# Order of the last second products, and the engines that copy and send the last rows, in a fused attention and ELU-MLP kernel

## The chip, the cores and the metric

The kernel runs on one core of one Trainium2 chip. The metric is the device time of one execution in microseconds (us); medians are over separate executions.

## The reference

The first half is sliding-window attention over 8 batches, 8 heads, 576 positions and 64 dimensions. The second is a two-layer MLP with an ELU between, on 4608 tokens:

```
x = attention(q, k, v)                  # window 32, softmax; (4608, 512)
h = x @ w_in                            # (4608, 2048)
g = where(h > 0, h, exp(min(h, 0)) - 1)
out = g @ w_out                         # (4608, 512) fp32
```

## The kernel before

The MLP runs in 144 steps: 18 tiles of 256 tokens, each in 8 steps of 256 hidden columns. One step is a first product (`mm1`, into PSUM), ScalarE's exponential, two VectorE operations that make g, and, two steps later, the second product (`mm2`), which adds into two PSUM tiles (the prediction says banks): `psY[t][0]` for the first 128 rows of the tile (called ts0 here, "upper rows") and `psY[t][1]` for the other 128 (ts1, "lower rows"). The attention is woven between the steps. In the very last step the first product is cut into two halves, so that g comes in two halves as well.

```python
def mm2(kk, parts=(0, 1)):
    t, s = order[kk]
    ...                                       # (cut) psY[t] allocated at s == 0
    for ts in parts:
        for j in range(FG):                   # FG = 2
            nc.tensor.matmul(psY[t][ts],
                lhsT=g_t[kk][:, j, ts * 128:(ts + 1) * 128],
                rhs=w_out_sb[:, s * FG + j, :], ...)
    if last and s == STEPS - 1:               # the last tile's rows
        for ts in parts:
            for z in range(1 + ts):           # ts0 whole, ts1 in two halves
                c = slice(z * D_MODEL // 2 * ts,
                          D_MODEL if z == ts else D_MODEL // 2)
                eng = (nc.vector, nc.scalar)[z]
                y_sb = opool.tile([128, D_MODEL], FP32,
                                  tag=f"y_sb{1 - z}", name="y_sb")
                copy_on(eng, y_sb[:, c], psY[t][ts][:, c])
                (nc.scalar if z else nc.sync).dma_start(
                    out_t[t, :, ts, c], y_sb[:, c])
    ...                                       # (cut) the other tiles' stores
```

The loop runs step 142's product in two parts, one part before each part of step 143's: 142 ts0, 143 ts0, 142 ts1, 143 ts1.

The softmax here doesn't subtract the row's maximum and nothing guards it: scores larger than these inputs give would overflow.

## Time and profile before

| | before |
|---|---|
| time, median of 3 runs | 305.11 us (304.83 to 305.93) |
| span of the profiled run | 304.5 us |
| TensorE busy | 296.0 us, 97% |
| start of ScalarE's last two exponentials to span end ("the tail", defined below) | 6.91 us |
| last packet of the stores to landing of the last store | 0.34 us |

The prediction below shows the engines' shares, the tail in order of time and the DMA engines' load. One part of the page that it does not show matters later. It is in the list of DMA queues over the whole span, of which these are the last three lines (packets, MB, share of 16 engines' time):

```profile
q10 hardware_dynamic: 1872, 6.62, 5.8%
q8 instruction: 24, 0.39, 0.6%
q14 instruction: 11, 0.09, 0.1%
```

q10 is ScalarE's queue; q1, left out here, is SyncE's (from 300.3 us on q10 moved 0.13 MB, ScalarE's one store of 128 KB, and q1 0.39 MB, SyncE's two). The packets of kind "instruction" I read as fetches of the engines' own program, since the experiments below move them by adding instructions to an engine (eight on ScalarE, one of q14 by some 6 us).

**A measure for the tail.** The body of the kernel scatters by some two microseconds from run to run (the moment at which the last step's first half exponential starts lay between 296.3 and 298.4 us in the 19 traces of this study). So all times of the tail are given from that moment, which I call the marker: the start of the first of ScalarE's last two 128x256 exponentials (297.56 us in this trace). "Tail" is from the marker to the end of the span.

### The profile page before, as it was taken

Reading aid. Unit: us, or ns where it says so; the run is one execution under the profiler, and the core shown is the slowest. Engines: PE = TensorE matmul, PEld = TensorE weight load, DVE = VectorE, ACT = ScalarE, POOL = GpSimd, SP = SyncE. Lnnn points to the kernel's source line nnn. Section 1 sums busy time; section 2 is a strip of 40 time slices with the busy share of each in tenths; the row PEclk is TensorE's granted clock in tenths of the full one; section 3 lists DMA queues with packets and bytes.
Section 4 is the critical chain, followed back from the end, with each engine's and each line's share of the span. In section 5 each row is a group of like instructions: output and inputs, shape, how many; then the busy total and the mean of one; then the engine's idle time right before and its main releaser. Section 6 shows DMA issues by size and latency. Waiting matters only on the chain.

```text
span 304.5 us, 7644 instructions
## 1 busy us (share of the span) xinstructions
PE 296.0 (97%) x3091; PEld 197.4 (65%) x3091; DVE 242.2 (80%) x473; ACT 168.6 (55%) x254; POOL 48.6 (16%) x68
## 2 busy tenths in 40 slices
PE   8789999999999999999999999999999999999995
PEld 3456666677676666666666666666667666666662
DVE  6867688978888887988798879887988787877664
ACT  3654556778664567546754675467535353534331
POOL 8836100910003100230013001400000000000000
PEclk9999999999999999999999999999999999999999
DMA  9999999998755997999799969996921111111011
GB/s 191 177 201 205 183 272 413 295 168 182 177 176 158 297 126 187 246 319 157 164 251 303 196 157 268 325 159 116 281 57 71 34 71 34 72 37 69 2 69 70
DMA packets 92117, 52.81 MB, mean 173 GB/s; under 512 B 76594, under 2 KB 81970, under 8 KB 92082
## 3 DMA queue, kind: packets, MB, share of 16 engines
q1 hardware_dynamic: 47330, 35.61, 43.3%
q0 software_dynamic: 42880, 10.10, 40.9%
q10 hardware_dynamic: 1872, 6.62, 5.8%
q8 instruction: 24, 0.39, 0.6%
q14 instruction: 11, 0.09, 0.1%
HBM read 36.70 MB, written 15.34 MB: 171 GB/s over the span
## 4 chain that ended last, share of the span: by engine, by line
PE 90%; DMA 3%; DVE 2%; POOL 2%; ACT 1%; issue 1%; DVEq 0%; POOLq 0%; ACTq 0%
PE ps L602 41%; PE psY L640 40%; PE psS L336 4%; PE psS L304 3%; DMA w_in_sb<-in_moe_w_in_dram 3%; PE ptx L279 1%; POOL Ve L142 1%; POOL c L136 1%; PE psXT L357 1%; DVE g_sb L626 1%; ACT pu L315 1%; DVE pm L324 0%; DVE m_sb L615 0%; PE ptx L274 0%; ACT e_sb L609 0%
## 5 line engine op out<-in xcount | busy, mean ns | idle before, releaser
L609 ACT ACTIVATE e_sb<-ps 128x512 f32<-128x512 f32 (+1 forms) x145 | 86.3, 595 | 120.6 <-PE ps L602 113.0
L602 PE MATMUL ps<-xT,w_in_sb 128*128 128x256 bf16 x1152 | 149.2, 273 | 1.4 <-DMA w_in_sb<-in_moe_w_in_dram 1.4
L640 PE MATMUL psY<-w_out_sb,g_sb 128*128 128x512 bf16 x576 | 147.6, 380 | 0.2 <-DVE g_sb L626 0.2
L602 PEld LDWEIGHTS <-w_in_sb 128*128 128x128 bf16 x1152 | 110.6, 98 | 39.7 <-DMA w_in_sb<-in_moe_w_in_dram 1.9
L626 DVE SCALAR_TENSOR_TENSOR g_sb<-ps,m_sb 128x512 bf16<-128x512 f32 (+1 forms) x145 | 99.4, 686 | 12.6
L615 DVE TENSOR_SCALAR m_sb<-e_sb 128x512 bf16<-128x512 f32 x144 | 62.5, 434 | 38.3 <-ACT e_sb L609 36.5
L640 PEld LDWEIGHTS <-g_sb 128*128 128x128 bf16 x576 | 54.5, 98 | 39.0 <-DVE g_sb L626 0.6
L142 POOL DMA_DIRECT2D Ve<-in_v_dram x40 | 35.4, 897 | 139.7 <-PE psS L336 79.9
L315 ACT ACTIVATE pu<-psS 128x1024 bf16<-128x1024 f32 x36 | 36.5, 1021 | 1.4 <-PE psS L304 1.4
L348 DVE TENSOR_TENSOR x_st<-psS,rc 128x512 bf16<-128x512 f32 x36 | 24.9, 692 | 1.2
L324 DVE TENSOR_TENSOR pm<-pu,masks 128x1024 bf16<-128x1024 bf16 x36 | 24.6, 683 | 0.6 <-ACT pu L315 0.5
L234 ACT CAST qkb<-f 128x768 bf16<-128x768 f32 (+1 forms) x29 | 25.0, 860 | 0.0
L336 PEld LDWEIGHTS <-pm 128*64 128x64 bf16 x576 | 11.2, 111 | 9.9 <-DVE pm L324 8.7
L336 PE MATMUL psS<-Ve,pm 128*64 128x65 bf16 x320 | 13.6, 197 | 0.9 <-DVE pm L324 0.9
L236 DVE COPY y_sb<-psY 128x512 f32<-128x512 f32 (+1 forms) x19 | 12.7, 671 | 1.0 <-PE psY L640 1.0
L304 PEld LDWEIGHTS <-kT 64*128 64x128 bf16 x576 | 9.5, 95 | 4.9 <-issue 4.0
L336 PE MATMUL psS<-Vo,pm 128*64 128x65 bf16 x256 | 12.0, 196 | 0.2 <-DVE Vo L153 0.2
L304 PE MATMUL psS<-qT,kT 64*128 64x64 bf16 x576 | 11.8, 191 | 0.5 <-DVE kT L236 0.5
L234 ACT COPY y_sb<-psY 128x512 f32<-128x512 f32 (+1 forms) x18 | 10.3, 571 | 3.0 <-DVE y_sb L236 3.0
L153 DVE COPY Vo<-Ve 64x1040 bf16<-64x1040 bf16 x24 | 10.3, 431 | 1.5 <-DMA Ve<-in_v_dram 0.8
L395 PE MATMUL ps_idle<-zeros 128*128 128x512 bf16 x27 | 9.5, 482 | 1.3 <-DVE zeros L194 1.3
L234 ACT COPY qT<-ptx 128x1152 bf16<-128x1152 bf16 (+2 forms) x8 | 7.5, 971 | 3.9 <-PE ptx L279 3.0
(36 smaller groups left out, 72.4 us busy)
## 6 DMA issues: line engine op xcount, KB each, us to landing
out_dram<-y_sb SPq DMA_DIRECT2D x35, 256.0 KB, 3.5
f<-in_q_dram SPq DMA_DIRECT2D x12, 576.0 KB, 5.6
f<-in_k_dram SPq DMA_DIRECT2D x12, 576.0 KB, 7.9
in_dram<-qkb ACTq DMA_DIRECT2D x10, 576.0 KB, 3.9
Ve<-in_v_dram POOLq DMA_DIRECT2D x24, 128.0 KB, 11.0
w_in_sb<-in_moe_w_in_dram POOLq DMA_DIRECT2D x4, 512.0 KB, 9.9
w_out_sb<-in_moe_w_out_dram POOLq DMA_DIRECT2D x4, 512.0 KB, 12.8
Ve<-in_v_dram POOLq DMA_DIRECT2D x16, 96.0 KB, 10.5
```

Source lines behind the costliest of these rows:

```text
L142: nc.gpsimd.dma_start(out=V_e[b % 3][p0:p1, m, :, 0:D], in_=v[b, :, lo + p0:lo + p1, :].rearrange("h p d -> p h d"))
L234: nc.scalar.copy(d_, s_)
L304: nc.tensor.matmul(psS[:, h % 2, hp * 128 + z * QB:hp * 128 + (z + 1) * QB], lhsT=kT[b % 2][base:base + 64, KPAD + hp * S + QB * qb - WIN: ...
L315: nc.scalar.activation(pu, _bap(psS, [psS.ap[0], [1, 1024]]), AX.Exp, scale=SCALE)
L324: nc.vector.tensor_mul(pm, pu, _bap(mm, [mm.ap[0], [0, H], [1, 2 * QB]]))
L336: nc.tensor.matmul(psS[QB * z:QB * (z + 1), par, hp * VD:(hp + 1) * VD], lhsT=pm[:, par * HP + hp, z * QB:(z + 1) * QB], rhs=vv[:, qb // 2 ...
L348: nc.vector.tensor_mul(x_st, _bap(psS, [psS.ap[0], [VD, HP], [512, 2], [1, D]]), _bap(rc, [rc.ap[0], [2, HP], [1, 2], [0, D]]))
L602: nc.tensor.matmul(ps[:, j, :], lhsT=w_in_sb[:, do, fo * 128:(fo + 1) * 128], rhs=xT[t][:, :, do, :], start=(do == 0), stop=(do == NDO - 1))
L609: nc.scalar.activation(e_sb, ps, AX.Exp)
L615: nc.vector.tensor_scalar(m_sb, e_sb, -1.0, None, ALU.add)
L626: nc.vector.scalar_tensor_tensor(g_t[kk][:, z * w:(z + 1) * w, :], ps, 0.0, m_t[kk][z], ALU.max, ALU.min)
L640: nc.tensor.matmul(psY[t][ts], lhsT=g_t[kk][:, j, ts * 128:(ts + 1) * 128], rhs=w_out_sb[:, s * FG + j, :], start=(s == 0 and j == 0), sto ...
```

## The change

The intent: PE does the last two second products in the plain order of steps, so that the wait for the last half of g falls behind more work; and of the lower rows ScalarE copies and sends the first half while VectorE, which is still busy with the upper rows, takes the second half.

```diff
-    def mm2(kk, parts=(0, 1)):
+    def mm2(kk):
...
-            for ts in parts:
-                for z in range(1 + ts):
-                    c = slice(z * D_MODEL // 2 * ts,
-                              D_MODEL if z == ts else D_MODEL // 2)
-                    eng = (nc.vector, nc.scalar)[z]
-                    y_sb = opool.tile([128, D_MODEL], FP32,
-                                      tag=f"y_sb{1 - z}", name="y_sb")
-                    copy_on(eng, y_sb[:, c], psY[t][ts][:, c])
-                    (nc.scalar if z else nc.sync).dma_start(
-                        out_t[t, :, ts, c], y_sb[:, c])
+            half = D_MODEL // 2
+            for ts, c0, n, z in ((0, 0, D_MODEL, 1), (1, 0, half, 0),
+                                 (1, half, half, 1)):
+                y_sb = opool.tile([128, D_MODEL], FP32, tag=f"y_sb{z}",
+                                  name="y_sb")
+                copy_on((nc.scalar, nc.vector)[z], y_sb[:, c0:c0 + n],
+                        psY[t][ts][:, c0:c0 + n])
+                (nc.scalar, nc.sync)[z].dma_start(
+                    out_t[t, :, ts, c0:c0 + n], y_sb[:, c0:c0 + n])
...
-            if n < NSTEP - 2:
-                mm2(n)
-            elif n == NSTEP - 1:
-                for ts in range(2):
-                    for m in (n - 1, n):
-                        mm2(m, (ts,))
+            mm2(n)
```

More of the change, by code (lines that the diff above doesn't have):

```diff
@@ L637, in mm2 @@
         last = t == NT - 1 and s == STEPS - 1
-        for ts in parts:
+        for ts in range(2):
             for j in range(FG):
@@ L646, in mm2 @@
         if last and s == STEPS - 1:
-            for ts in parts:
-                for z in range(1 + ts):
-                    c = slice(z * D_MODEL // 2 * ts,
-                              D_MODEL if z == ts else D_MODEL // 2)
-                    eng = (nc.vector, nc.scalar)[z]
-                    y_sb = opool.tile([128, D_MODEL], FP32,
-                                      tag=f"y_sb{1 - z}", name="y_sb")
-                    copy_on(eng, y_sb[:, c], psY[t][ts][:, c])
-                    (nc.scalar if z else nc.sync).dma_start(
-                        out_t[t, :, ts, c], y_sb[:, c])
+            half = D_MODEL // 2
[7 more added lines that the diff above has]
+                    out_t[t, :, ts, c0:c0 + n], y_sb[:, c0:c0 + n])
         elif s == STEPS - 1:
```

## The prediction

> **What bounds the kernel now.** I read the page first, then the chain of waits, and then, because the change touches only the last two second products and the last three stores, the timeline and the stretches of the last 7 us. The page says what the body is:
>
> ```profile
> span 304.5 us, 7644 instructions
> PE 296.0 (97%) x3091; PEld 197.4 (65%) x3091; DVE 242.2 (80%) x473; ACT 168.6 (55%) x254; POOL 48.6 (16%) x68
> PE 90%; DMA 3%; DVE 2%; POOL 2%; ACT 1%; issue 1%; DVEq 0%; POOLq 0%; ACTq 0%
> ```
>
> TensorE is busy 97% of the span and 90% of the chain that ends last. The change adds and removes no matmul, so all of the body up to the last few microseconds stays; only the tail can move. The tail, in order of time (start us, duration us, engine, line, operation; in brackets the idle time before and what ended it):
>
> ```profile
> 297.79 1.67 PE L640 MATMUL psY<-w_out_sb,g_sb 128*128 128x512 bf16 x7
> 299.14 0.42 DVE L626 SCALAR_TENSOR_TENSOR g_sb<-ps,m_sb 128x256 bf16<-128x256 f32 x1
> 299.62 0.76 PEld L640 LDWEIGHTS <-g_sb 128*128 128x128 bf16 x5 [0.64 <-DVE g_sb L626]
> 299.62 1.25 PE L640 MATMUL psY<-w_out_sb,g_sb 128*128 128x512 bf16 x5 [0.16 <-DVE g_sb L626]
> 300.05 0.69 DVE L236 COPY y_sb<-psY 128x512 f32<-128x512 f32 x1 [0.48 <-PE psY L640]
> 300.77 0.93 SPq L657 DMA_DIRECT2D out_dram<-y_sb  x2
> 300.91 0.42 DVE L236 COPY y_sb<-psY 128x256 f32<-128x256 f32 x1 [0.17 <-PE psY L640]
> 301.37 0.37 ACT L234 COPY y_sb<-psY 128x256 f32<-128x256 f32 x1 [3.00 <-DVE y_sb L236]
> 301.77 0.36 ACTq L657 DMA_DIRECT2D out_dram<-y_sb  x1
> ```
>
> The first row of matmuls is step 141 (4), the upper rows (ts0) of step 142 (2) and one of step 143. Then PE waits for the second half of the last g (ends 299.56), and does one more ts0 matmul and the four of the lower rows (ts1). The copy of ts0 starts after that first one; the two half copies of ts1 follow at 300.91 and 301.37. The chain of waits follows exactly these and ends with ScalarE's half copy: "301.37 0.37 ACT y_sb L234" is its last piece. It stops there because the stores' landing is no engine's work. But the span runs on to 304.46. What happens in between is in the stretches (PE, PEld, DVE, ACT, POOL busy with counts; then clock, DMA share, GB/s):
>
> ```profile
> 301.10:301.60 0.50, 0.00 (x0) 0.00 (x0) 0.24 (x1) 0.23 (x1) 0.00 (x0) 1.00 0.00 0
> 301.60:302.10 0.50, 0.00 (x0) 0.00 (x0) 0.00 (x0) 0.14 (x1) 0.00 (x0) 1.00 0.99 369
> 302.10:302.60 0.50, 0.00 (x0) 0.00 (x0) 0.00 (x0) 0.00 (x0) 0.00 (x0) 1.00 0.99 350
> 302.60:303.10 0.50, 0.00 (x0) 0.00 (x0) 0.00 (x0) 0.00 (x0) 0.00 (x0) 1.00 0.91 322
> 303.10:303.60 0.50, 0.00 (x0) 0.00 (x0) 0.00 (x0) 0.00 (x0) 0.00 (x0) 1.00 0.09 25
> ```
>
> This is the reading on which I stake the prediction. The first store (ts0, 256 KB, issued 300.77) moves its first packet at 301.60, and from then on all 16 DMA engines are full, without a gap, until about 303.05. The two 128 KB stores of ts1 never find an idle engine: their data queue behind ts0's. In the single packet records a 2048-byte packet takes 85 ns and a 1024-byte packet 45 ns, so each engine has 8 x 85 + 16 x 45 = 1400 ns plus three completion writes of 7 ns, about 1.42 us; 301.60 + 1.42 = 303.02, and with engines starting up to 0.1 us apart the last packet ends at 303.19. The last store lands at 303.53 and the closing barriers take 0.93 us more, to 304.46. So **the end = start of the first of the three stores + 0.83 us to its first packet + about 1.42 us of full DMA engines + receipt + barriers**. The finish of the last copy matters only if its store is ready after the engines run dry. It comes close: the ACT store, issued at 301.77, has its first packet at 302.66, just when the 680 + 360 ns of the two stores before it are through (302.65).
>
> [...]
> - [...] the share is 0.99 with one queue at work and does not rise with two.
> - [...] the trace shows 369 and 350 in the two full stretches[...].
> - [...] ScalarE's half copy indeed waits for VectorE's (the bracket of the 301.37 line), although both halves were ready together at 300.88. So the two halves of ts1 stay serial after the change too: swapping the order of the engines doesn't make them parallel.
> - [...] The trace: (1.67 - 0.38)/6 = 0.215 us, with 0.38 the duration of one.
>
> **The change part by part.**
> 1. *Order of the second products.* Before: 142 ts0, 143 ts0, 142 ts1, 143 ts1. After: 142 both, then 143 both. The twelve matmuls from 297.79 on are the same. Before, the wait for the last half of g left a hole: the eighth would have started at 297.79 + 7 x 0.215 = 299.30 and started at 299.62, 0.32 us later. After, the two ts1 matmuls of 142 (0.43 us) stand in front of it and fill the hole. The j=1 matmul of 143 ts0 is now the tenth: 297.79 + 9 x 0.2155 = 299.73, when g is already there (299.56 + 0.05). The twelfth starts at 300.16 and ends at 300.54, where before it ended at 300.87 (299.62 + 1.25). So **the last rows are ready 0.33 us earlier, but the first rows 0.11 us later** (299.73 in place of 299.62). This second part is what I think the intent overlooks.
> 2. *ts0 copy and store.* Still VectorE, still SyncE's queue: starts 300.05 + 0.11 = 300.16, ends 300.85 (0.69), store issued 300.88, first packet 301.71.
> 3. *First half of ts1, now ScalarE.* PE done 300.54; copy 300.58 to 300.95 (0.37, the duration of before); ACT store issued 300.98, 0.39 us before the second store of the kernel before (300.77 + 0.93 - 0.33 = 301.37). First packet possible at 300.98 + 0.89 = 301.87 (0.89 is what ACT's store took before).
> 4. *Second half, now VectorE.* It is free at 300.85, but the bank is ScalarE's until 300.95: 300.99 to 301.41 (0.42), SyncE store issued about 301.44, where the last issue was at 301.77: **0.33 us earlier**. First packet possible 302.27.
> 5. *Transfers.* Bytes and packet sizes are unchanged, 1.42 us per engine. The engines fill from 301.71: ts0 alone would last to 302.39; ACT's store is ready at 301.87 and stretches the work to 302.75; the last is ready at 302.27, well before that. No gap, so the last packet ends 0.11 us later than before, near 303.30, the landing near 303.64, the span about 304.57.
>
> Sum: +0.11 us at the first store, -0.33 us at the last issue, which is hidden in the DMA queue. Net +0.1 us on 305.11: **305.2 us**.
>
> **The rivals.**
> - *The last copy sets the end* (what the chain of waits suggests, and likely the intent). Then the 0.33 us count in full: 305.11 - 0.33 = 304.8 us. Against it: the full DMA share from 301.60 to 303.10. For it: the balance is close, since ACT's store was ready only when the engines came free. If its 0.89 us were a delay of its own and not partly queueing, something of a gain might be left, but not past the first store's later start.
> - *No movement at all*: if the later start of ts0 is eaten by something (for instance the weight load of the tenth matmul isn't late and the copy starts sooner than I count), time stays 305.1.
> - *Two queues at once cost more.* After, ACT's descriptors and packets fall into ts0's transfer. If their issue or the alternation of 2048- and 1024-byte packets cost a wait, perhaps 0.2 us more: 305.4. Against it: in the stretch where SyncE's and ACT's queues overlapped before (around 302.7) packets still took 45 ns.
> - *A real parallel copy of the two halves*, if the wait were not made here: VectorE would run 300.87 to 301.29. It would only bring forward a store that queues anyway: again 305.2.
>
> **Range and chances.** All rivals lie within 0.4 us of 305.11, which is 0.13%. Three runs of the kernel before spread from 304.83 to 305.93, 0.4%; this spread, and not the mechanism, sets my range: 304.6 to 305.9. A 2% change is 6.1 us, more than the whole tail after the last matmul (304.46 - 300.87 = 3.6 us). So faster 0.005, same 0.99, slower 0.005.
>
> **What would show it right or wrong.** Right: PE's twelve last matmuls without a hole, ending near 300.54; ts0's copy starting about 300.16 and not 300.05; ScalarE's half copy before VectorE's, with VectorE waiting a tenth of a microsecond for it; last issue near 301.44; DMA engines full from about 301.71 without a gap; span end 0.1 us later or equal. Wrong: a gap in the DMA share or packets slower than 45 and 85 ns, a last landing before 303.5, a ts0 copy at 300.05 or before, or a half copy that waits for something else. For the 2% verdict to be wrong, something before 297.8 us would have to move, and the diff touches nothing there.

## The result and the profile after

The changed kernel took **306.5 us** (median of 5 runs, 306.25 to 306.86) against 305.2 us of the kernel before (median of 5, 304.83 to 305.93). The ratio is 1.0041, with a 95% interval from 1.0024 to 1.0057. Ratios here are the mean time of one kernel's runs over that of the other's from the same rounds, so they are not quite the ratio of the quoted medians. By the 2% rule this is "same", but it is a real loss of about 1.3 us, outside the predicted range (304.6 to 305.9).

The tail in order of time, in the trace of after (columns as in the prediction):

```profile
297.09 0.82 ACT L609 ACTIVATE e_sb<-ps 128x256 f32<-128x256 f32 x2 [0.70 <-PE ps L602]
...
297.55 2.54 PE L640 MATMUL psY<-w_out_sb,g_sb 128*128 128x512 bf16 x11
...
299.69 1.26 DVE L236 COPY y_sb<-psY 128x512 f32<-128x512 f32 x2 [0.59 <-PE psY L640]
300.12 0.37 ACT L234 COPY y_sb<-psY 128x256 f32<-128x256 f32 x1 [2.21 <-PE psY L640]
300.41 0.90 SPq L656 DMA_DIRECT2D out_dram<-y_sb  x2
300.52 0.36 ACTq L656 DMA_DIRECT2D out_dram<-y_sb  x1
```

The marker is at 297.09, so subtract that. PE runs without a hole to 2.99 us after the marker (300.08), where it was 3.32 before; the row shows 11 matmuls of the twelve, since some matmul records are missing from a trace (the page of after counts 3038 matmuls and 3091 weight loads; before had 3091 of both). The ts0 copy starts at 2.60 (before: 2.49), and the last store is issued at 3.88 (before: 4.22). All of this is as predicted to a hundredth or two. The work of the engines ends earlier than before, and still the kernel is slower. So the time was lost after the last issue. The DMA engines' load (columns as in the prediction):

```profile
301.24:301.74 0.50, 0.00 (x0) 0.00 (x0) 0.00 (x0) 0.00 (x0) 0.00 (x0) 1.00 0.96 360
301.74:302.24 0.50, 0.00 (x0) 0.00 (x0) 0.00 (x0) 0.00 (x0) 0.00 (x0) 1.00 0.99 350
302.24:302.74 0.50, 0.00 (x0) 0.00 (x0) 0.00 (x0) 0.00 (x0) 0.00 (x0) 1.00 0.95 320
302.74:303.24 0.50, 0.00 (x0) 0.00 (x0) 0.00 (x0) 0.00 (x0) 0.00 (x0) 1.00 0.09 31
303.24:303.74 0.50, 0.00 (x0) 0.00 (x0) 0.00 (x0) 0.00 (x0) 0.00 (x0) 1.00 0.00 0
```

From 301.24 on the engines are full for 1.5 us, as before. In the stretch before the last something small remains, then nothing. What remains is told by the queues and the stores' landings from 300 us on (the first block is queue: packets, MB, share; the second is queue and kind, size, us from issue to landing):

```profile
q1 hardware_dynamic: 288, 0.39, 22.2%
q10 hardware_dynamic: 144, 0.13, 8.0%
q14 instruction: 1, 0.01, 0.4%
...
out_dram<-y_sb SPq DMA_DIRECT2D x1, 256.0 KB, 2.0
out_dram<-y_sb ACTq DMA_DIRECT2D x1, 128.0 KB, 2.3
out_dram<-y_sb SPq DMA_DIRECT2D x1, 128.0 KB, 3.1
```

The last store needs 3.1 us from issue to landing. The same lines of before, from 300.3 us on:

```profile
q14 instruction: 1, 0.01, 0.7%
...
out_dram<-y_sb SPq DMA_DIRECT2D x1, 128.0 KB, 1.8
out_dram<-y_sb ACTq DMA_DIRECT2D x1, 128.0 KB, 1.8
```

There the two stores of that size took 1.8 us. In the single packet records of the trace of after the stores' data are through at 302.90. At that moment a packet of 8192 bytes of queue 14 starts, an instruction fetch, and it takes 309 ns of one DMA engine (the 0.4% in the lines of after, of 16 engines' 4.9 us, are 0.31 us). The last completion write (4 bytes) of the last store starts at 303.21, when that packet ends, and the store lands only at 304.05, another 0.84 us later. The three stores of each tail have 48 4-byte packets, and each of their three semaphores gets 16 increments, so I read these packets as completion writes, one for each increment. A store has landed with the sixteenth: SyncE's check of the last store's semaphore runs 0.02 us after it (6.00 us after the marker in before, 6.98 in after). Of the last store in after, 15 came by 6.09 us after the marker and the sixteenth at 6.96; in before all 16 came between 5.81 and 5.98. So one completion write of the 16 was late, which I read as one DMA engine alone.

In before there is one such fetch packet too, but it starts at 303.37, after the last packet of the stores (303.19), and the last store lands 0.34 us after its last packet.

So the two tails compare as follows, from the marker:

| | before | after |
|---|---|---|
| PE's last matmul ends | 3.32 | 2.99 |
| first store's first packet | 4.04 | 4.14 |
| last store issued | 4.22 | 3.88 |
| instruction fetch starts | 5.81 | 5.81 |
| last packet of the stores | 5.64 | 6.12 |
| last store landed | 5.98 | 6.96 |
| end of span | 6.91 | 7.89 |

The tail has grown by 0.98 us, which is most of the 1.3 us between the medians.

### The profile page after: what moved, and what is told of

The parts are those of the page before. It is cut to its first block, busy times and chain, and to the rows that moved or that the text cites. A ratio compares the mean times of both kernels' runs of the same rounds, so it can differ in the third digit from the quotient of the medians. Undisturbed runs are those within 1.5% of the kernel's fastest.

```text
span 305.0 us, 7591 instructions
## 1 busy us (share of the span) xinstructions
PE 291.5 (96%) x3038; PEld 197.2 (65%) x3091; DVE 242.1 (79%) x473; ACT 168.8 (55%) x254; POOL 48.7 (16%) x68
## 4 chain that ended last, share of the span: by engine, by line
PE 89%; DMA 3%; POOL 2%; DVE 2%; issue 2%; ACT 1%; POOLq 0%; DVEq 0%; ACTq 0%
PE ps L602 41%; PE psY L640 39%; PE psS L336 4%; PE psS L304 3%; DMA w_in_sb<-in_moe_w_in_dram 3%; PE ptx L279 1%; POOL Ve L142 1%; POOL c L136 1%; PE psXT L357 1%; ACT pu L315 1%; DVE pm L324 0%; DVE g_sb L626 0%; PE ptx L274 0%; DVE Vo L153 0%; PE ps_idle L395 0%
## 5 line engine op out<-in xcount | busy, mean ns | idle before, releaser
L640 PE MATMUL psY<-w_out_sb,g_sb 128*128 128x512 bf16 x526 | 139.1, 379 | 3.1 <-issue 0.8
L395 PE MATMUL ps_idle<-zeros 128*128 128x512 bf16 x24 | 8.3, 453 | 1.4 <-DVE zeros L194 1.3
```

The source lines that it names most:

```text
L640: nc.tensor.matmul(psY[t][ts], lhsT=g_t[kk][:, j, ts * 128:(ts + 1) * 128], rhs=w_out_sb[:, s * FG + j, :], start=(s == 0 and j == 0), sto ...
```

## The experiments

**Theory FETCH**: the loss is an instruction fetch of ScalarE that runs on one DMA engine in front of the last store's completion. Why ScalarE: four of the eleven queue-14 packets of before, at 54.27, 135.38, 209.96 and 303.37 us, come when ScalarE's records in the trace number 65, 194, 322 and 447. That is nearly one per 128 records, or 64 bytes of the packet's 8192 for each. The other seven seem to be other engines' (see after_dve8). **Rivals**: TWO QUEUES (SyncE's and ScalarE's stores under way together make the receipt late) and CHANCE (tails scatter). Seventeen kernels ran. All gave correct results. The measures of their tails, in us from the marker, are in one table; the text after it goes through them.

| kernel | first packet | last packet of stores | fetch starts | last store landed | tail |
|---|---|---|---|---|---|
| before_again | 4.04 | 5.63 | 6.08 | 5.97 | 6.89 |
| before_act8 | 4.04 | 5.63 | -0.29 | 5.97 | 6.90 |
| before_act2 | 4.05 | 6.20 | 5.08 | 6.60 | 7.53 |
| copies_act8 | 4.04 | 5.64 | -0.30 | 5.98 | 6.91 |
| copies_only | 4.04 | 5.64 | 5.63 | 6.15 | 7.08 |
| order_act8 | 4.15 | 5.75 | -0.04 | 6.10 | 7.09 |
| order_only | 4.15 | 5.74 | 5.62 | 6.08 | 7.07 |
| after_again | 4.15 | 6.13 | 5.77 | 6.92 | 7.84 |
| after_dve8 | 4.15 | 6.13 | 5.78 | 6.92 | 7.85 |
| after_act8 | 4.14 | 5.75 | -0.28 | 6.09 | 7.01 |
| after_act2 | 4.15 | 6.05 | 4.03 | 6.38 | 7.31 |
| after_minus2 | 4.14 | 5.74 | 7.51 | 6.08 | 7.01 |
| quarters_after | 3.88 | 6.70 | -0.29 | 7.05 | 8.40 |
| quarters_before | 3.78 | 6.59 | -0.28 | 6.94 | 8.29 |
| quarters2_after | 3.89 | 5.62 | -0.29 | 5.97 | 7.32 |
| quarters2_before | 3.78 | 5.59 | -0.28 | 5.93 | 7.28 |
| three_stores | 3.89 | 5.70 | -0.29 | 6.04 | 6.97 |

### Does it come again, and is it the fetch?

The first four ran on one chip in the same rounds. No edit in before_again:

> The kernel before, unchanged, for a second trace and the span of every run. Measure used in all runs: the tail, from the start of the last step's first half exponential (ACT e_sb, 128x256, the first of the last two) to the span's end; it was 6.91 us in the trace of before and 7.89 us in that of after. Theory FETCH: in the trace of after an 8192-byte instruction-fetch packet (queue 14) ran on one DMA engine from 302.90 to 303.21, the completion write of the last store on that engine came behind it (303.21) and the store landed only at 304.05, where the last data had ended at 302.90; in the trace of before the same fetch started at 303.37, after the last packet (303.19). FETCH expects a tail of 6.9 us again, last store landing 0.35 us after its last packet, fetch after it. Rival TWO QUEUES: the late landing comes of the SyncE and ScalarE stores being under way together, fetch or not; it also expects 6.9 here. Rival CHANCE: tails scatter by a microsecond from run to run; then 6.9 needn't come again.

Measured: 305.49 us (median of 6, 305.14 to 306.75) against 305.3 us (11 runs), ratio 1.0003 (0.9984 to 1.0022). Tail 6.89, as expected.

No edit in after_again:

> The changed kernel, unchanged, on the same chip. FETCH and TWO QUEUES: tail 7.9 us again within 0.15, the last store landing about 3.1 us after its issue (2.0 or less for the others), time 0.9 to 1.3 us over the kernel before. CHANCE: tail anywhere between 6.9 and 7.9, and time within 0.5 us of before.

Measured: 306.5 us (5 runs, 305.98 to 306.86), ratio 1.0031 (1.0013 to 1.0050). Tail 7.84, last landing 3.03 us after issue. CHANCE falls: two traces of each kernel agree within 0.05 us.

Now the fetch is moved. Eight tiny ScalarE instructions go into ScalarE's idle start (in after it runs nothing from 3.93 to 6.27 us):

```diff
     nc.scalar.activation(warm, zeros[:, 0:1], AX.Exp)
+    for _ in range(8):
+        nc.scalar.copy(warm, zeros[:, 0:1])
```

> The changed kernel with eight one-column copies more on ScalarE in its idle start, so that every later instruction fetch of ScalarE (every 128 instructions, 8192 bytes) comes eight ScalarE instructions earlier, some 4 to 6 us. FETCH: the last queue-14 packet falls before 300 us, the last store lands about 0.35 us after its last packet, tail 7.0 to 7.1 us (0.1 to 0.2 over before, from the later first store and the interleaving), time 0.7 to 0.9 us below after_again. TWO QUEUES: tail stays 7.9, time as after_again. If the fetch isn't ScalarE's, it doesn't move and neither does the time.

Measured: 305.65 us (5 runs, 305.12 to 305.91), ratio 1.0002 (0.9986 to 1.0019), 0.85 us under after_again. The stores from 300 us on, in the trace of after_act8:

```profile
q1 hardware_dynamic: 288, 0.39, 25.8%
q10 hardware_dynamic: 144, 0.13, 9.0%
...
out_dram<-y_sb SPq DMA_DIRECT2D x1, 256.0 KB, 2.1
out_dram<-y_sb ACTq DMA_DIRECT2D x1, 128.0 KB, 2.3
out_dram<-y_sb SPq DMA_DIRECT2D x1, 128.0 KB, 2.2
```

The queue-14 line is gone: the fetch came 0.28 us before the marker. The last store lands in 2.2 us, with SyncE's and ScalarE's stores under way together just as in after, and ScalarE's has the same 2.3 us in both. So TWO QUEUES falls. Tail 7.01.

The same eight instructions in the kernel before:

> The kernel before with the same eight copies. It tells whether the eight copies themselves cost or gain anything: FETCH expects tail 6.9 us and the time of before within 0.3 us, with the fetch gone from the end (in before it fell behind the last packet and delayed nothing). TWO QUEUES and CHANCE expect no change either.

Measured: 305.81 us (6 runs, 305.16 to 306.96), ratio 1.0010 (0.9991 to 1.0030), tail 6.90. The instructions themselves cost and gain nothing that can be seen.

As a control, eight on VectorE in place of ScalarE, in the changed kernel (`nc.vector.tensor_copy(warm_v, zeros[:, 0:1])`, eight times at the same place):

> The changed kernel with eight one-column copies more at the start, on VectorE and not on ScalarE. FETCH: ScalarE's count of instructions is as in after, so its fetch stays in the tail near 5.8 us in front of the last completion write, tail 7.8 to 7.9 us. If eight instructions anywhere (a shifted start) had been what mended after_act8: tail 7.0.

Tail 7.85, fetch at 5.78. It is ScalarE's count, not a shifted start. The trace also tells whose the other packets are: five that lay at 35.65, 93.68, 148.54, 204.15 and 259.63 us in after now come 2.7 to 4.5 us earlier, while the rest, ScalarE's four among them, moved by 0.8 us at most. So queue 14 seems to carry VectorE's fetches too.

### Which half of the change?

With the fetch out of the way (eight copies), the two halves of the change one at a time. order_act8 is the kernel before with this edit:

```diff
-            if n < NSTEP - 2:
-                mm2(n)
-            elif n == NSTEP - 1:
-                ...
+            mm2(n)
```

> The kernel before with the change's order of the second products alone (142 both, 143 both; the copies and stores of before), and the eight early ScalarE copies that take the instruction fetch out of the tail. FETCH with the prediction's arithmetic: the hole on PE is filled, ts0's copy starts 0.11 us later (2.60 us into the tail, 2.49 before), the DMA engines fill 0.10 later, tail 7.0 us. If the last issue set the end: 0.33 us less, 6.6 us.

Tail 7.09, first packet at 4.15, ts0's copy at 2.60. The landing moved by +0.12 us (6.10 against 5.98), as the later first store wants; the other 0.06 us fell in the closing checks after it. The last issue, 0.16 us earlier than before (4.05 against 4.22), bought nothing.

copies_act8 is the kernel before with the change's table of copies (ScalarE first half, VectorE second) and the old order:

> The kernel before with the change's copies and stores alone (ScalarE first half, VectorE second; the order of products of before), and the eight early copies. FETCH: first store as before, transfers gapless, last issue as before: tail 6.9 us. If two queues under way together cost receipts: 7.0 or more with the last SyncE store landing later than 2.2 us after its issue.

Tail 6.91, the same as before. The exchange of engines alone does nothing.

The same two without the eight copies, so with the fetch back in the tail:

> The order alone, without the eight copies: the fetch of ScalarE is back in the tail. Data end about 5.74 us into the tail (5.63 before); the fetch began at 5.77 to 6.08 in the traces so far. FETCH expects 7.0 us if the fetch falls behind the last packet of its DMA engine and about 7.8 if it falls in front of it; the trace must show the one with the other. TWO QUEUES expects no late landing (ScalarE's store comes last here, and nothing else is under way by then): 7.0.

> The new copies and stores alone, without the eight copies. Data end about 5.65; FETCH expects the fetch behind it and a tail of 6.9 (or 7.7 with the fetch in front, if ScalarE's earlier finish, by 0.46 us, brings its fetch forward: that would show that the copies' half of the change is what moved the fetch). TWO QUEUES expects about 7.7 here with the fetch behind.

order_only 7.07, the same as with the fetch moved (it started at 5.62, on an engine whose last store was not held up, since that store landed at 6.08). copies_only 7.08, which is 0.17 more than copies_act8: the fetch started at 5.63, about when the last packet ended, and the landing came 0.17 later. This landing is late without a late packet; I take it for the same meeting of fetch and completion at its edge (0.51 us from the last packet to the landing, 0.34 in copies_act8), but only this one trace shows it. Neither half alone makes the loss of 0.9 us. It takes the order (data 0.1 us later) and the copies (ScalarE through earlier) together.

### Where the fetch falls decides

Two early ScalarE copies and not eight bring the fetch only a little forward. In the kernel before:

> The kernel before with two ScalarE copies more at the start and not eight: the fetch is asked for two ScalarE instructions earlier, about 0.8 us (near ScalarE's last half copy in place of its drain), while the last store is still to be issued. If an early request of the fetch is what hurts in the changed kernel (there ScalarE drains 3.83 us into the tail, 4.62 in before), this slows the kernel before: a late landing of the last store (over 2.2 us after its issue) and a tail of 7.3 to 7.8 us. If the fetch waits for the engines to run dry anyway, tail 6.9 with the fetch behind.

The fetch ran at 5.08, the last store landed 2.39 us after its issue, tail 7.53. So the tail of the kernel before, with its good order, becomes 0.63 us longer through two instructions that run some 290 us earlier. (The time of this one run, 305.55 us, can't show it: the body scatters by more.) The load of the DMA engines at the end of that trace:

```profile
301.80:302.30 0.50, 0.00 (x0) 0.00 (x0) 0.00 (x0) 0.00 (x0) 0.00 (x0) 1.00 0.14 45
302.30:302.80 0.50, 0.00 (x0) 0.00 (x0) 0.00 (x0) 0.00 (x0) 0.00 (x0) 1.00 0.02 8
```

and its queues and landings from 299 us on:

```profile
q14 instruction: 1, 0.01, 0.6%
...
out_dram<-y_sb SPq DMA_DIRECT2D x1, 128.0 KB, 2.5
out_dram<-y_sb ACTq DMA_DIRECT2D x1, 128.0 KB, 2.4
```

The marker is at 296.31; the other engines are done at some 301.9, and the trickle at a share of 0.02 is what a single late engine makes (1/16 for 0.2 of 0.5 us is 0.025): its packets end at 302.51. The semaphores agree: of each of the last two stores 15 increments came by 5.61 and 5.97 us after the marker, and the sixteenth at 6.29 and 6.60. The two last stores land in 2.5 and 2.4 us, where before had 1.8.

In the changed kernel:

> The changed kernel with two early ScalarE copies and not eight: the fetch is asked for two ScalarE instructions earlier (about 0.8 us) than in after, so it runs while every DMA engine has plenty of data left. FETCH: what costs is the position in front of the last store's data or completion; an engine that fetches amid its data is 0.31 to 0.5 us late and nothing more, as in before_act2 (last store landed 2.39 us after its issue): tail 7.3 to 7.5, between after_act8 (7.0) and after (7.9). If any fetch in the tail costs 0.8: 7.8.

Fetch at 4.03, before the first data, 686 ns; data ends at 6.05 and the last store lands in 2.5 us, tail 7.31. So a fetch amid or ahead of the data costs 0.3 us here (0.6 in before_act2), and the one right in front of the last completion costs 0.9. What makes it 0.3 in one kernel and 0.6 in the other is open.

The other way: SyncE issues the two first loads that ScalarE issued, so ScalarE has two instructions fewer:

```diff
-        load_qk(0, which, HALF_A, (nc.sync, nc.scalar))
+        load_qk(0, which, HALF_A, (nc.sync, nc.sync))
```

> The changed kernel with the two first loads that ScalarE issued now issued by SyncE: two ScalarE instructions fewer, so the fetch is asked for later or not at all before the end. FETCH: fetch behind the last packet or absent, tail 7.0. If the fetch's time is tied to the tail and not to ScalarE's count: fetch at 5.8 again, tail 7.9. The start of the kernel may be slower by the serial loads; only the tail is read.

Tail 7.01, the fetch at 7.51, 0.50 us after the end of the span. (The time of 307.16 us is that of a slower start: the marker came at 298.41 us.) So removing instructions mends the tail just as adding eight does.

### Can the first store be brought forward?

The prediction's formula says that the end hangs on the first store. I cut ts0 into two half copies and two half stores, with the eight early copies in place:

```diff
-            for ts, c0, n, z in ((0, 0, D_MODEL, 1), (1, 0, half, 0),
-                                 (1, half, half, 1)):
+            for ts, c0, n, z in ((0, 0, half, 1), (0, half, half, 1),
+                                 (1, 0, half, 0), (1, half, half, 1)):
```

> The changed kernel with the eight early copies, and ts0 copied and sent in two halves by VectorE and SyncE, so that the first store starts after 0.42 us of copying and not 0.69. The prediction's formula (end = first packet + 1.42 us of full engines) expects the first packet 0.27 us earlier than in after_act8 (3.87 us into the tail, 4.14), a gap of about 0.1 us before the second, and a tail of 6.8 us (7.0 in after_act8, 6.9 in before). If the last issue set the end now: 7.0.

> The order of products of before, the copies of the change, the eight early copies, and ts0 in two halves. First packet at 3.77 us, but the last rows' half copies end at 4.18, so the last store is ready at 5.0 and ends at 5.4: tail 6.75 us. If it is the last issue that binds here: 6.9.

Measured: 306.92 us (6 runs, ratio 1.0043, 1.0028 to 1.0059) and 306.89 us (6 runs, ratio 1.0047, 1.0026 to 1.0067), both slower. This was my own fault: the third VectorE tile under one tag, with two buffers, waited for the first store to land. VectorE's last copy started at 4.90 in place of 3.43. Mended, by giving the second half of ts0 the other tag's buffers:

```diff
-                y_sb = opool.tile([128, D_MODEL], FP32, tag=f"y_sb{z}",
+                y_sb = opool.tile([128, D_MODEL], FP32, tag=f"y_sb{z if ts or not c0 else 0}",
```

> quarters_after mended: there VectorE's last half copy took the buffer of the first store and waited for its landing (started 4.90 us into the tail in place of 3.43), so it tested that wait and not the formula. Here the second half of ts0 has the other buffer pair. Formula (end = first packet + 1.42 us of full engines + 0.1 of skew): first packet 3.88, a gap of under 0.1, last packet 5.5, tail 6.8 us (after_act8 7.01, before 6.90). If the last issue (3.89, unchanged from after_act8) set the end: 7.0. Time: 0.1 us under before, within noise.

> The same mending with the order of products of before. First packet 3.78; the last store, issued at 4.22, is ready at 5.05 and needs 0.36 us: last packet 5.45 to 5.5, tail 6.75 us. Here the last issue binds and no longer the transfers, so no more than 0.15 us under before.

Measured: 305.86 us (5 runs, ratio 1.0008, 0.9989 to 1.0026) and 305.69 us (5 runs, ratio 1.0007, 0.9992 to 1.0022). The last landing came at 5.97 and 5.93, earlier than in after_act8 (6.09), by less than expected. The tails are longer even so, 7.32 and 7.28: the fourth store got a completion semaphore which SyncE's closing checks wait for second in their fixed order, and seven further checks of some 0.06 us each came after the landing. In after_act8 those had been made while the stores ran. So the last version has three stores again:

```diff
+            rows = [opool.tile(..., tag=f"y_sb{ts}") for ts in range(2)]
+            for ts, c0, z, s0 in ((0, 0, 1, 0), (0, half, 1, half),
+                                  (1, 0, 0, None), (1, half, 1, 0)):
+                copy_on((nc.scalar, nc.vector)[z], ...)     # a half row block
+                if s0 is not None:
+                    nc.sync.dma_start(out_t[t, :, ts, s0:c0 + half], ...)
```

> The change's order, the eight early ScalarE copies, and three stores, all on SyncE: first half of ts0, second half of ts0, whole ts1 (ScalarE copies its first half, VectorE its second). In quarters2_after the last store landed 5.97 us into the tail (6.09 in after_act8), but a fourth store took a fourth completion semaphore that SyncE's closing checks wait for early in their order, with seven more waits (0.45 us) still behind it; with three stores these stand before the landing again. Formula: first packet 3.88, last store issued about 3.89, its first packet possible 4.72 and 0.68 us long, last packet 5.45 to 5.55, landing 5.8 to 5.9, tail 6.75 to 6.85 us (before 6.90, after_act8 7.01). If the closing waits or a slower store take it back: 7.0 or more. Time 0.1 us below before, not to be told apart by five rounds.

Measured: 305.32 us (5 runs, 305.24 to 305.37) against 305.53 us (9 runs), ratio 0.9991 (0.9978 to 1.0005). The tail is 6.97, not 6.75 to 6.85. The load shows why:

```profile
300.80:301.00 0.20, 0.00 (x0) 0.00 (x0) 0.00 (x0) 0.00 (x0) 0.00 (x0) 1.00 0.50 159
301.00:301.20 0.20, 0.00 (x0) 0.00 (x0) 0.00 (x0) 0.00 (x0) 0.00 (x0) 1.00 1.01 348
301.20:301.40 0.20, 0.00 (x0) 0.00 (x0) 0.00 (x0) 0.00 (x0) 0.00 (x0) 1.00 0.78 246
301.40:301.60 0.20, 0.00 (x0) 0.00 (x0) 0.00 (x0) 0.00 (x0) 0.00 (x0) 1.00 0.75 282
```

The engines run dry between the stores (shares of 0.50, 0.78 and 0.75): the small first store is through before the second is ready, and the last one is issued at 3.96 with its first packet at 4.87. Once the first store is early, the issues bind and the rule "end = first packet + 1.42 us" no longer holds. It beats the changed kernel, but nearly all of that is the eight copies: the tail of after_act8 is 7.01. That it beats the kernel before is not shown, since the interval includes 1.

## Why the prediction was wrong

**Its steps 1 to 4 held.** Relative to its marker (297.555 us unrounded), it had PE's last matmul end at 2.99 (measured 2.99), ts0's copy start at 2.61 (2.60), ScalarE's half copy at 3.03 to 3.40 (3.03 to 3.40), VectorE's at 3.44 to 3.86 (3.43 to 3.86), and the last issue at 3.89 (3.88). VectorE waited for ScalarE, as it said: in after its half copy waits for the semaphore that ScalarE's copy raises, and started 0.03 us after that copy's end.

**The step that failed is 5, "Transfers".** It read: "No gap, so the last packet ends 0.11 us later than before, near 303.30, the landing near 303.64, the span about 304.57." From the marker these are 5.75, 6.09 and 7.02. The changed kernel had 6.12, 6.96 and 7.89. What stood in their place is an instruction fetch of ScalarE: the step counted only the three stores as users of the DMA engines. The packet was in the profile of before, as one q14 packet in the last stretch (at 502 ns it is 0.06 of that stretch's share of 0.09) that I quoted and did not ask about.

**With the fetch out of the way, step 5 is right to a few hundredths.** after_act8 has 5.75, 6.09 and 7.01. The interval of its ratio (0.9986 to 1.0019) contains the predicted +0.1 us, though five rounds can't tell 0.1 us from nothing. order_act8 and copies_act8 show where the 0.1 us comes from: the order, through the later ts0, and not the exchange of engines.

**Why the fetch met the stores only in the changed kernel.** ScalarE's last instructions come earlier there: its drain (the first of the closing instructions) started 3.83 us after the marker, against 4.62 in before. In before ScalarE was the last to issue, and its fetch began 0.17 us after the last packet of the stores (5.81 against 5.64). That before escaped was luck: in before_act2 two small instructions undo it. The fetch followed that drain by 1.2 us in before, 1.5 in before_again and copies_only, 1.2 in order_only, and 1.9 to 2.0 in the traces of after. That it is requested near ScalarE's end fits; why it starts so late in after, just as the data runs out, is open. The trace doesn't name the DMA engine of a packet or show when a fetch is requested; that fetch and late completion share an engine is read from their times and from the single late increment.

**What the 0.9 us consist of.** The packet itself is 0.31 us, and by 0.30 us the completion write was late (in after the stores' data are through 5.81 us after the marker, and the write starts at 6.11). Another 0.5 us is a later receipt: 0.84 us from the completion write to the landing against 0.34 in before. In after, after_again and after_dve8, where the fetch is directly ahead, the landing follows the last packet of the stores by 0.79 to 0.84 us. But in copies_only the last completion write ended at 5.64, when the fetch had just begun (5.63), and that landing was late too, 0.51 us after the write. Why the receipt is later beside a fetch was not shown: no run isolates it.

**The rivals.** "The last copy sets the end" is refuted: order_act8 and after_act8 issue earlier and end later. "Two queues at once cost more" had the right sign and the wrong cause: with the fetch gone, both queues under way together cost nothing beyond the 0.1 us. Of the loss of about 1.3 us (1.2 in the second set of rounds), 0.95 to 0.98 us are in the tail. The rest lies within the body's scatter and is not explained.

**The range.** It was built from the spread of the kernel before and not from what could be wrong with step 5. My widest rival was +0.2 us, a guess that no trace stood behind.

## What to carry to other kernels

When a tail of a few microseconds is worked out from DMA load, list every queue that is active there, not only your own: an 8 KB instruction fetch in front of the last completion cost 0.9 us here. Eight early copies on the engine whose program it brings moved it from 5.81 to -0.28 us, and two instructions fewer moved it to 7.51; before crediting or blaming a reordering of the tail, make that shift in both kernels and compare. And while the stores filled the DMA engines here (shares of 0.94 to 0.99 in after_act8), the first store's start counted (its first packet 0.10 us later, the tail 0.11 longer than in before_act8) and the last copy's end did not (the last store issued 0.33 us earlier, without gain), until the first was so early that the engines ran dry between issues (shares of 0.50 to 0.78 in three_stores).

## Figures that these traces give

- Fetches: those of queue 8 have 16384 bytes, those of queue 14 have 8192, ScalarE's coming nearly every 128 of its records (65, 194, 322, 447 in before). The one in the tail took 309 ns in after, 502 ns in before and 686 ns in after_act2, and one that met the last store lengthened the tail by 0.88 us (7.89 in after against 7.01 in after_act8).
- Receipts: a completion write right behind a fetch landed after 0.84 us in after, where it was 0.34 us in before; the cause is not shown.
- First packet: in before it came 0.83 us after the start of the issue on SyncE's queue (0.50 after the issue's end).
- Closing checks: SyncE waits for the completion semaphores one after another, in the same order of numbers in before and after, about 0.06 us each (six from 4.19 to 4.49 us after the marker in before). A store whose semaphore stood early in that order had seven checks behind it in quarters2_after, which cost some 0.4 us (the tail was 1.35 us longer than the last landing there, 0.92 in after_act8).
